# A fused SSM-convolution and gMLP block on one core: the order of work at the passage into the MLP is made anew, and two GpSimd residuals wait for VectorE's first two normalized tiles

## The chip, the cores and the metric

The kernel runs on one core of a Trainium2 chip. A core has five engines with a queue of instructions each: TensorE (PE; its weight loads are shown apart as PEld), VectorE (DVE), ScalarE (ACT), GpSimd (POOL) and SyncE (SP), which here only issues DMAs. The metric is the device time of one execution in microseconds (us). Of a kernel three executions are timed and the median is taken; one more execution is profiled, and its trace is what is read below.

## The reference

The computation is one block with a modulation vector, 2048 positions of 640 channels, in bf16. Cut to what matters:

```python
mod = (silu(c) @ w_mod).reshape(1, 6, 1, -1)          # sa, ca, ga, sb, cb, gb
h = layernorm(x) * (1 + ca) + sa
x = x + ga * A(h, k, v, shift_k, ssm_k, ssm_D)        # short conv of k, times v, long convolution by FFT, times h
h = layernorm(x) * (1 + cb) + sb
x = x + gb * B(h, w_in, w_sp, b_sp, w_out)            # gMLP

def B(x, w_in, w_sp, b_sp, w_out):
    z = gelu(x @ w_in)                                 # 640 -> 1728
    z1, z2 = z[..., :864], layernorm(z[..., 864:])
    g = w_sp @ z2 + b_sp                               # 2048 x 2048 over positions
    return (z1 * g) @ w_out                            # 864 -> 640
```

## The kernel before

The work has three stretches. The first computes part A. The 640 channels are taken in five blocks of 128 (`u` = 0 to 4), the long convolution is a two-stage FFT by matmuls, and every block ends with a product into `gh` and a residual `xt += gh`. The last stretch computes the position mixing (w_sp) and the output projection of part B. Between them lies the passage into the MLP, which the change concerns. Positions are taken there in 16 tiles of 128, four tiles to a group `g`.

For a group the passage does this. The last channel block's outputs arrive from TensorE (`yl`, L875, matmuls of 16 columns). VectorE multiplies them into `gh` (`yml`, L879) and adds `gh` to `xt` (`res`, L831). VectorE takes statistics of `xt` (`ln2`, L837; `ag2`, L968), GpSimd raises the variance to the power -1/2 (`rstd2`, in group 0 `rstdq`, L238), and the tiles are normalized into `Z` (`zx`, L984 to L988, on VectorE, ScalarE or GpSimd). Group 0 goes in two halves of two tiles each; its tiles are turned by TensorE (`hfl`, L1002), five 128x128 blocks a tile, and scaled and shifted out of PSUM by `hmod` (L1014 on ScalarE, L1016 on VectorE). The other groups are turned by a DMA (L1034) and modulated in place (`hmod2`, L1040 and L1042). Then TensorE multiplies by w_in (`zz`, L1060, five accumulating matmuls of 432 columns for each of four outputs of a tile), and ScalarE takes the gelu (L1066) and, for groups 0 and 1, the sum of squares (`zsq`, L1077).

Every operation is recorded with a number; nothing is emitted until the whole program has been recorded. What sets the order is then the table `ORDER` (L51 to L118), written out: each entry is an engine's letter and an operation's number, and `Plan.run` (L149) emits them in this order, so that each engine's queue has its own entries in the order of the table. Tiles' buffers are given out in the same order. Waits between engines follow from what operations read and write. One kind of entry adds a wait: `H` is GpSimd with a gate. A gated operation also waits for the last VectorE operation ahead of it in the table whose kind is in the set `PORT` (L39):

```python
            if e == "D" and o["kind"] in PORT:
                held = made[-1]
            elif gated and held is not None:
                tc.add_manual_dep(made[0], held.name, mybir.DependencyInfo(mybir.DependencyClass.Sync, mybir.DependencyReason.SCHED_ONLY), reason="port")
```

The numbers that matter here: 702 and 759 are the residuals of channel blocks 3 and 4 for group 1 (tiles 4 to 7); 754 is the residual of channel block 4 for tiles 2 and 3; 783 and 784 normalize tiles 0 and 1; 782 is GpSimd's power ahead of them; 785 and 786 are the turns of tiles 0 and 1; 787 to 791 are the `hmod` of the first half; 812, 805, 810 and 829 are the first four groups of `zz` matmuls; 757, 771 and 764 are `yl` of groups 1, 3 and 2. 1040, 1046, 1047 and 1048 are fills (L1112): matmuls of 512 columns whose result nobody reads, two in 1040 and one in each of the others. 590 and 597 are small matmuls for the modulation vector gb. 862 is one of the five `hmod2` of group 1.

## Time and profile before

| | |
|---|---|
| time, median of 3 runs | 303.22 us (303.2 to 303.69) |
| profiled execution: its own time | 303.96 us |
| profiled execution: span, from first to last instruction | 302.2 us |
| PE busy | 292.3 us (97%) |
| VectorE busy | 258.0 us (85%) |
| ScalarE busy | 166.7 us (55%) |
| GpSimd busy | 168.2 us (56%) |
| mean granted TensorE clock | 0.989 of full speed |

A busy share is a mean over stretches with different limits. In the profile's rows an instruction stands with its start in us from the span's start, its duration, its engine, line, operation, what it writes and reads, and, in brackets, how long its engine stood idle before it and what ended that. Rows of equal instructions are merged (x3). Durations of instructions that follow each other overlap by their latency, so that the distance of starts is the better price of one.

### The profile page before, as it was taken

How to read it: one execution, taken by the hardware profiler on the slowest of the kernel's cores; microseconds unless marked ns; L12 is line 12 of the kernel's file. 1: busy time of each engine (PE TensorE's matmuls, PEld its weight loads, DVE VectorE, ACT ScalarE, POOL GpSimd, SP SyncE). 2: the span in 40 equal slices, each digit the busy share in tenths (PEclk: the TensorE clock that was granted, in tenths of full speed). 3: DMA queues.
4: the chain of work that ended last, by engine and by line, in shares of the span. 5: the costliest groups of instructions: out<-in, count | busy, mean ns of one | idle time of the engine just before them, and what ended most of it. 6: DMA issues, size and time to landing. Idle time of an engine off the chain costs nothing.

```text
span 302.2 us, 7173 instructions
## 1 busy us (share of the span) xinstructions
PE 292.3 (97%) x2833; PEld 207.1 (69%) x2833; DVE 258.0 (85%) x541; ACT 166.7 (55%) x325; POOL 168.2 (56%) x192
## 2 busy tenths in 40 slices
PE   6799999999999999799999999999999999999996
PEld 3689999999999988655555555555555555665664
DVE  8999999999998999979887877977678787687895
ACT  6899999997898866159789578310111102111110
POOL 3652768938767988554520521067841655487850
PEclk9999999999999999779999999999999999999999
DMA  8999789995466978005596930049756547332424
GB/s 161 284 230 275 154 221 264 133 229 144 91 121 116 280 126 276 2 2 104 152 209 126 188 74 1 0 90 172 141 138 85 103 112 161 83 85 74 102 68 128
DMA packets 117155, 41.57 MB, mean 138 GB/s; under 512 B 102557, under 2 KB 117122, under 8 KB 117122
## 3 DMA queue, kind: packets, MB, share of 16 engines
q1 hardware_dynamic: 116968, 41.08, 62.6%
q8 instruction: 22, 0.36, 0.5%
q14 instruction: 11, 0.09, 0.1%
q10 hardware_dynamic: 154, 0.05, 0.1%
HBM read 16.60 MB, written 2.63 MB: 64 GB/s over the span
## 4 chain that ended last, share of the span: by engine, by line
PE 90%; DVE 7%; issue 1%; ACT 1%; POOL 0%; DVEq 0%; POOLq 0%
PE ps L1172 24%; PE pu L295 22%; PE pz L295 18%; PE sm L295 7%; PE po L1381 7%; PE s L295 5%; PE po L1394 3%; PE pz L1172 2%; PE pu L1172 1%; DVE Tf L515 1%; DVE T L396 1%; PE sm L654 1%; PE sm L423 1%; DVE st L837 1%; DVE xt L831 1%
## 5 line engine op out<-in xcount | busy, mean ns | idle before, releaser
L295 PEld LDWEIGHTS <-Z 128*128 128x128 bf16 x320 | 31.7, 100 | 28.0 <-issue 1.7
L295 PE MATMUL pu<-X,M 128*128 128x128 bf16 (+1 forms) x480 | 46.2, 237 | 0.4 <-DVE Tf L515 0.3
L529 POOL TENSOR_TENSOR W<-Tf 128x256 bf16<-128x256 f32 x42 | 30.1, 734 | 17.2 <-DVE Tf L515 8.6
L1172 PEld LDWEIGHTS <-S 128*128 128x128 bf16 x256 | 25.0, 98 | 20.8
L295 PEld LDWEIGHTS <-M 128*128 128x128 bf16 x480 | 36.5, 98 | 3.1 <-issue 0.7
L298 ACT CAST X<-s 128x1024 bf16<-128x1024 f32 x32 | 32.7, 1022 | 2.8 <-PE s L295 2.6
L295 PE MATMUL pu<-big,Z 128*128 128x432 bf16 x160 | 33.6, 353 | 0.0
L295 PE MATMUL pz<-big,Z 128*128 128x432 bf16 x160 | 33.5, 353 | 0.0
L515 DVE TENSOR_TENSOR Tf<-pu,KH 128x1024 f32<-128x1024 f32 x25 | 30.4, 1218 | 0.8 <-ACT Z L298 0.4
L1172 PEld LDWEIGHTS <-wT 128*128 128x128 bf16 x192 | 18.8, 98 | 15.3
L1178 ACT COPY m<-ps 128x432 f32<-128x432 f32 x7 | 3.6, 517 | 46.1 <-PE ps L1172 46.1
L295 PEld LDWEIGHTS <-G 128*128 128x128 bf16 x330 | 25.0, 98 | 1.9 <-issue 0.3
L298 ACT CAST KH<-pu 128x512 bf16<-128x512 f32 x40 | 23.5, 605 | 4.2 <-PE pu L295 3.6
L298 ACT CAST Z<-pz 128x512 bf16<-128x512 f32 (+1 forms) x41 | 23.3, 587 | 4.3 <-PE pz L295 4.2
L1172 PE MATMUL ps<-X,wT 128*128 128x432 bf16 x112 | 22.7, 346 | 0.0
L1172 PE MATMUL ps<-X,S 128*128 128x432 bf16 x112 | 22.6, 346 | 0.0
L1172 PE MATMUL ps<-T,S 128*128 128x432 bf16 x112 | 22.2, 346 | 0.0
L1180 ACT ACTIVATE m<-ps,bcol 128x432 f32<-128x432 f32 x7 | 4.3, 621 | 30.2 <-PE ps L1172 30.2
L295 PEld LDWEIGHTS <-X 128*128 128x128 bf16 x288 | 17.8, 98 | 4.4 <-issue 1.8
L295 PE MATMUL sm<-dg,big 128*128 128x128 bf16 x320 | 20.5, 219 | 0.0
L515 DVE TENSOR_TENSOR T<-pu,KH 128x1024 bf16<-128x1024 f32 x15 | 18.3, 1220 | 2.3 <-PE pu L295 2.2
L295 PEld LDWEIGHTS <-big 128*128 128x128 bf16 x320 | 18.8, 98 | 0.3
(235 smaller groups left out, 668.5 us busy)
## 6 DMA issues: line engine op xcount, KB each, us to landing
wm<-in_w_mod_dram SPq DMA_DIRECT2D x6, 800.0 KB, 5.0
xt<-in_A_q_dram SPq DMA_DIRECT2D x4, 640.0 KB, 5.9
out_dram<-ot SPq DMA_DIRECT2D x15, 160.0 KB, 2.0
big<-in_B_w_in_dram SPq DMA_DIRECT2D x2, 1080.0 KB, 8.1
X<-in_A_ssm_k_dram SPq DMA_DIRECT2D x4, 512.0 KB, 7.3
ZT<-in_A_v_dram SPq DMA_DIRECT2D x1, 1024.0 KB, 7.7
big<-in_A_v_dram SPq DMA_DIRECT2D x1, 1024.0 KB, 7.8
w_o<-in_B_w_out_dram SPq DMA_DIRECT2D x6, 160.0 KB, 2.9
```

The lines of the kernel that those rows point to most:

```text
L295: nc.tensor.matmul(o, lhsT=w, rhs=x, start=start, stop=stop)
L298: (e.copy if e is nc.scalar else e.tensor_copy)(dst, src)
L396: e.tensor_scalar(tl[a][:, h], tl["mbase"][:], mstep[:, h * NCH + i:h * NCH + i + 1], MAGIC, op0=ALU.add, op1=ALU.add)
L423: e.transpose(pt[:, i, :], flatM[:, 8 * b + i, :], ident[:])
L515: e.tensor_tensor(T_[:], (tl[pu] if src is None else tl[src])[:, :, :, None, :].to_broadcast(shape), tl[KH][:, :, None, :, :].to_broadcast ...
L529: e.tensor_tensor(tl[W][:, :, o, :], T_[:, :, 0, o, :], T_[:, :, 1, 1 - o, :], op=ALU.add if o else ALU.subtract)
L654: e.transpose(p_[:, i, :], tl[kvt][:, c0 + i, :], ident[:])
L1172: nc.tensor.matmul(ps[:, :FC], lhsT=lhs[:, s_, :], rhs=rhs(s_), start=(s_ == 0 and not more), stop=(s_ == HT - 1), skip_group_check=more)
L1178: e.copy(part[p, m][:], part[p, BANK[m]][:, :FC])
L1180: e.activation(part[p, m][:], part[p, BANK[m]][:, :FC], ACT.Identity, bias=T["bcol"][:, p + HT:p + HT + 1], scale=1.0)
L1381: nc.tensor.matmul(ps[:, :HS], lhsT=w(k), rhs=x(k), start=start and k == 0, stop=stop and k == n - 1, skip_group_check=True)
L1394: e.matmul(po[t, i][:, :hi - lo], lhsT=uTs[t][:fsz[ft], ft, :], rhs=T["w_o"][:fsz[ft], ft, lo:hi], start=(ft == 0), stop=(ft == NFT - 1))
```

## The change

Only the table `ORDER` changes. In three groups of lines between the last channel block and the second group of the MLP, entries are put in another order; two of them also change their letter, from `G` to `H`: 702 stands behind D783 now, and 759 behind D784. Those two are of the kind `zx`, which is in `PORT`, so residual 702 waits for the normalization of tile 0 and residual 759 for that of tile 1. Of the diff a few lines, since its rows only list numbers:

```diff
@@ ORDER @@
-P731 P737 D740 G677 P727 D732 D738 D698 P741 P743 P746 P748 D699 P745 P744 A728 P747 P742 D749 D750 D751 P1046 P1047
-P1048 D752 P757 D780 P1040 S589 D781 P590 D753 D758 D754 P771 G782 D783 D784 G702 D756 A591 P597 A598 D701 P785 P786
-D787 A791 A790 D788 P764 D789 G759 P812 D755 D700 D793 D792 D704 P805 A813 D705 D762 S779 P829 D724 A806 G794 D795
+P731 P737 D740 G677 P727 D732 D738 D698 P741 P743 P746 P748 D699 P745 P744 A728 P747 P742 D749 D750 D751 P1046 P757
+P1047 P1048 D752 D780 S589 D781 P590 D753 D758 D754 P771 G782 D783 H702 D784 H759 D756 A591 P597 P1040 A598 D701 P785
+P786 D787 A790 A791 D788 P764 D789 P812 D755 D700 D793 D792 D704 P805 A813 D762 S779 D724 A806 D763 G794 D795 D761
...
-A828 D768 D707 D769 D708 D653 D710 D654 S599 S858 P820 A821 A809 P825 A826 D859 D860 D861 A832 P817 D863 D909 A814
+A828 D768 D707 D769 D708 D653 D710 D654 S599 S858 P820 A821 P825 A826 A809 D859 D860 D861 A832 P817 P833 A818 A834
```

On GpSimd at the residuals of group 1 the rows ahead and behind keep their order; `rstd` is the power -1/2, and the semaphores that an instruction waits for stand in brackets. Before:

```order
L831 TENSOR_TENSOR xt<-xt,gh 128x4x128
L238 TENSOR_TENSOR rstd_83<-mv_82,mhalf 128x2 [waits DVE_49]
L831 TENSOR_TENSOR xt<-xt,gh 128x4x128
L831 TENSOR_TENSOR xt<-xt,gh 128x4x128 [waits DVE_49]
L236 TENSOR_SCALAR rstd_83<-mv_82 128x2 [waits DVE_49]
L238 TENSOR_TENSOR rstd_83<-rstd_83,mhalf 128x2 [waits Pool_49]
```

And now:

```order
L831 TENSOR_TENSOR xt<-xt,gh 128x4x128
L238 TENSOR_TENSOR rstd_83<-mv_82,mhalf 128x2 [waits DVE_49]
L831 TENSOR_TENSOR xt<-xt,gh 128x4x128 [waits DVE_49] x2
L236 TENSOR_SCALAR rstd_83<-mv_82 128x2 [waits DVE_49]
L238 TENSOR_TENSOR rstd_83<-rstd_83,mhalf 128x2 [waits Pool_49]
```

The first residual behind the power had no wait of its own; now both wait for VectorE, the first for 783 and the second for 784.

On TensorE ahead of the turns of tiles 0 and 1 (L1002, `Z`): `vcol` is operation 597, `s<-ident` with 512 columns a fill, `wm` the small matmuls of operation 590. Before, the two fills of 1040 stand ahead of 590:

```order
L295 MATMUL pz<-Ebd,X 128x4x4
L295 LDWEIGHTS ident
L295 MATMUL s_2843<-ident 128x512
L295 LDWEIGHTS wm
L295 MATMUL sm<-sc_bf,wm 128x1
...
L295 LDWEIGHTS vcol
L295 MATMUL sm<-ident,vcol 5x128
L1002 LDWEIGHTS Z
L1002 MATMUL s_2924<-ident,Z 128x128
```

And now they stand directly ahead of the turns:

```order
L295 LDWEIGHTS vcol
L295 MATMUL sm<-ident,vcol 5x128
L295 LDWEIGHTS ident
L295 MATMUL s_2919<-ident 128x512
L1002 LDWEIGHTS Z
L1002 MATMUL s_2925<-ident,Z 128x128
```

The 32 matmuls of 757 have moved ahead of two of the three single fills, and the pair 1040 has moved behind 597.

On VectorE a few statistics change places around the residuals' readers (`gsa_bf` is an addition into `gh`; `nmr` is the bias for the second half's normalization), and one `hmod2` of group 1, 862, comes over from ScalarE:

```order
 L968 BN_AGGR mv_82<-st_72 128x2 x2
-L837 BN_STATS st_72<-xt 128x6 x3
-L776 TENSOR_TENSOR gh<-gh,gsa_bf 128x4x128
+L837 BN_STATS st_72<-xt 128x6 x2
+L776 TENSOR_TENSOR gh<-gh,gsa_bf 128x4x128
+L837 BN_STATS st_72<-xt 128x6
 L974 SCALAR_TENSOR_TENSOR nmr_84<-mv_82,rstd_83 128x2
...
-L1042 TENSOR_SCALAR Z<-Z,cb_col,sb_col 128x4x128 x4
+L1042 TENSOR_SCALAR Z<-Z,cb_col,sb_col 128x4x128 x5
```

One of the three statistics ahead of the addition now stands behind it, and the in-place modulation of group 1 is five rows of VectorE instead of four. On TensorE 810 also goes ahead of 829, and on ScalarE gelus and sums of squares of group 0 and 1 change places among themselves. No instruction is added or removed.

## The prediction, written before the changed kernel ran

> **What bounds the kernel now.** The page comes first: the granted clock by slices of 7.6 us, and what the chain that ended last consists of.

> ```profile
> span 302.2 us, 7173 instructions
> ...
> PEclk9999999999999999779999999999999999999999
> PE 90%; DVE 7%; issue 1%; ACT 1%; POOL 0%; DVEq 0%; POOLq 0%
> ```

> TensorE sets the end nearly everywhere. The 7% of VectorE are a place where TensorE waits, and the clock falls in just two slices, from 121 to 136 us. So the second view is the chain of waits in order of time around there.

> ```profile
> 124.11 1.23 DVE xt L831
> 125.34 1.20 DVE Z L988
> 126.54 0.05 issue
> ...
> 127.84 0.84 PE sm L295 x32
> 128.68 1.81 PE pz L295 x5
> 130.49 3.63 PE pu L295 x15
> 134.13 0.17 PE s L1002 x3
> ...
> 134.68 2.74 PE pz L295 x15
> ...
> 145.63 0.91 PE pu L295 x5
> ```

> Behind these 0.05 us of issue the chain stays on TensorE until its last matmul, so a microsecond won there is one at the end if no input becomes late. Two losses stand in these rows. The first: fifteen `zz` matmuls take 3.63 us (0.242 each) at 130.49 and 2.74 us (0.183 each) at 134.68. The second: VectorE's residual and normalization take 1.23 and 1.20 us. The third view, the timeline by engine, shows what is unusual in that.

> ```profile
> 121.99 0.29 DVE L831 TENSOR_TENSOR xt<-xt,gh 128x256 bf16<-128x256 bf16 x1
> 124.11 1.23 DVE L831 TENSOR_TENSOR xt<-xt,gh 128x256 bf16<-128x256 bf16 x1
> 125.27 1.62 DVE L988 TENSOR_SCALAR Z<-xt,mv,rstd 128x640 bf16<-128x640 bf16 x2
> 148.31 1.51 DVE L988 TENSOR_SCALAR Z<-xt,mv,rstd 128x640 bf16<-128x640 bf16 x4
> 124.04 2.31 POOL L831 TENSOR_TENSOR xt<-xt,gh 128x512 bf16<-128x512 bf16 x2
> 126.59 0.50 PE L1002 MATMUL s<-ident,Z 128*128 128x128 bf16 x3 [1.64 <-DVE Z L988]
> ```

> The same residual took 0.29 us at 121.99, when GpSimd was idle, and 1.23 at 124.11. Two normalizations should take 0.76 (1.51 us for four) and took 1.62. GpSimd's two residuals (702 and 759) ran from 124.04 to 126.35, right behind the power, 1.16 us each. VectorE's residual ended as the first of them did (125.2), and the first normalization as the second. GpSimd holds something that both engines need for a whole instruction, and TensorE stands idle for 1.64 us. The fourth view is the granted clock by stretches.

> ```profile
> 118.53:121.94 3.41, 3.36 (x67) 2.81 (x65) 3.27 (x9) 2.23 (x4) 2.69 (x3) 1.00 0.54 191
> 121.94:125.36 3.42, 3.01 (x94) 2.55 (x91) 3.32 (x11) 0.42 (x2) 2.00 (x3) 1.00 0.02 5
> 125.36:128.77 3.41, 2.18 (x43) 2.05 (x44) 3.10 (x8) 0.84 (x2) 0.99 (x1) 0.50 0.00 0
> 128.77:132.18 3.41, 3.41 (x11) 1.45 (x10) 3.41 (x15) 0.80 (x3) 2.07 (x4) 0.50 0.00 0
> ```

> The clock (ahead of the last two columns) is half for two stretches of 3.41 us, 125.36 to 132.18. What came before it:

> ```profile
> 121.35 0.81 PE L295 MATMUL s<-ident 128*128 128x512 bf16 x3
> 122.00 0.95 PE L295 MATMUL pz<-Ebd,X 128*128 128x16 bf16 x32
> 122.80 0.59 PE L295 MATMUL s<-ident 128*128 128x512 bf16 x2
> 123.23 0.76 PE L295 MATMUL sm<-sc_bf,wm 128*128 128x1 bf16 x25
> 123.86 0.94 PE L295 MATMUL pz<-Ebd,X 128*128 128x16 bf16 x32
> ```

> At full clock 432 columns take 0.183 us, 0.42 ns each. In 121.94 to 125.36 stand 64 x 16, 2 x 512, 25 and 128 columns (the `vcol` turn): 2,201 columns, 0.93 us, 27% of the stretch, although TensorE counts as busy for 3.01 of it. My reading is that the clock follows what streams through in such a stretch: after 27% it fell.

> **The change part by part.** *The held residuals.* 702 and 759 no longer start behind the power but behind normalizations 783 and 784. Residual 754 then takes 0.29 instead of 1.23 (124.11 to 124.40), and the normalizations 0.38 each: 783 ends at 124.83, 784 at 125.20. With the 0.05 us of issue seen at 126.54, the turns of tile 0 can start at 124.88 and those of tile 1 at 125.25. Before, tile 0's began at 126.59, and tile 1's normalization ended at 126.89 (125.27 + 1.62). Does 702 get between 783 and 784? It is released at 783's end plus some 0.08, at 124.91, and 784 has issued by 124.79, so I take 784 first; the other end is a rival below. The new waits cost nothing there: 702 runs 125.2 to 126.35, 759 to 127.5. Behind them on GpSimd stands the power for the second half.

> ```profile
> 126.81 0.60 DVE L837 BATCH_NORM_STATS2 st<-xt 128x6 f32<-128x128 bf16 x2
> 127.72 1.05 DVE L1016 TENSOR_SCALAR Z<-s,cb_col,sb_col 128x256 bf16<-128x256 bf16 x3 [0.31 <-issue]
> 129.66 0.19 POOL L236 TENSOR_SCALAR rstd<-mv 128x2 f32<-128x2 f32 x1 [3.31 <-DVE mv L968]
> 127.93 1.02 ACT L1014 ACTIVATE Z<-sm,sb_col,cb_col 128x256 bf16<-128x256 bf16 x2 [2.68 <-PE sm L1002]
> 132.85 0.91 ACT L984 ACTIVATE Z<-xt,nmr,rstd 128x640 bf16<-128x640 bf16 x1
> ```

> That power waited 3.31 us for VectorE; 1.9 us earlier it would start at 127.8, behind 759's 127.5. VectorE's readers of the two residuals (statistics of tiles 4 to 7) come about 128.0. Does GpSimd now hold up the `hmod` of the first half, from 125.8 on? They read PSUM. The gauge is VectorE's copies out of PSUM at 119.26 beside two GpSimd residuals:

> ```profile
> 119.26 1.31 DVE L298 COPY X<-pz 128x512 bf16<-128x512 bf16 x3
> 119.42 2.27 POOL L831 TENSOR_TENSOR xt<-xt,gh 128x512 bf16<-128x512 bf16 x2 [0.47 <-DVE gh L793]
> ```

> 0.42 us each, no stretching, so nothing below; the upper bound is that the hmods wait until 127.5, 1.7 us, which gives the gain back.

> *TensorE's rows ahead of the turns.* 1040 moves behind 597. With `yl` 757 earlier, 757, two fills, 590, 771 and 597 end at 121.57 + 0.80 + 0.43 + 0.63 + 0.80 + 0.06 = 124.3, by the distances of starts above, and the two fills at 124.73, 0.15 before the turns may start. So they cost nothing; without that cover at most 0.43 us. They do change the stretch 121.94 to 125.36: 4 x 512, 49 x 16, 153 and about seven turns of 128 are 3,900 columns, 1.64 us, 48% instead of 27%.

> *The sum with the clock kept.* Turns of tile 1 from 125.25 at 0.056 a block (0.17 for three at 134.13): done 125.53. `hmod`: VectorE has its two statistics until 125.80, then three at 0.35, until 126.85; ScalarE's two 125.62 to 126.65. `yl` 764: 0.84, until 126.4. The first `zz` group's third matmul waits for 126.85, and the group ends at 126.9 + 3 x 0.183 = 127.45, before at 130.49. Then fifteen at 0.183: 130.2, before 134.13. **Gain 3.9 us.** Kept in sight for the second half: the power there (127.8) and VectorE's bias behind it let ScalarE's normalization of tile 2 start at about 129.1, and with its 0.91 it ends at 130.0, so TensorE's arrival at 130.2 just holds.

> *The sum with the clock lost again* from 125.36. For one stretch: turns end 125.7, `yl` 126.55, five matmuls at 0.363 until 128.4, one more, then fourteen at 0.183: 131.3, gain 2.8. For two, until 132.18: ten and a half at 0.363, the rest at 0.183: 133.0, gain 1.1.

> Which? 48% lies between 27%, after which the clock fell, and the stretch ahead of it, 118.53 to 121.94, after which it did not. Its groups (the view by lines, for that stretch alone):

> ```profile
> L853 PE MATMUL pu<-ident,Z 128*128 128x128 bf16 x16 | 1.6, 219 | 0.0
> L853 PE MATMUL pz<-ident,Z 128*128 128x128 bf16 x16 | 1.5, 219 | 0.0
> L295 PE MATMUL sm<-Ebd,X 128*128 128x16 bf16 x32 | 1.1, 170 | 0.0
> ```

> Of these 32 turns four began before the stretch; 28 x 128, 32 x 16 and the three fills of 121.35 are 5,632 columns, 69%. I take kept, since the lowest stretch anywhere in the new order stays at about 40%, at some distance from 27%.

> [...]

> *What is moved besides.* 810 ahead of 829, and gelus and squares among themselves: same work on engines that follow TensorE, nothing. 862 costs VectorE another 0.34 (four took 1.37) and spares ScalarE one instruction:

> ```profile
> 143.17 1.37 DVE L1042 TENSOR_SCALAR Z<-Z,cb_col,sb_col 128x512 bf16<-128x512 bf16 x4
> ```

> Group 1's first matmul at 145.63 needs them. VectorE is 1.9 us early at its first `hmod` (125.80 for 127.72) and waits less at the second turns, up to 3.9; I take 3.2, an estimate between these. Then it comes to 143.17 at 140.0, and five end at 141.7; TensorE comes at 141.7, and needs the fourth 0.55 later. No loss, but little left. No DMA moves in its queue.

> **The rivals.** *Clock lost for one stretch*: 303.96 - 2.8 = 301.2. For it: the limit lies unseen between 27 and 69%. *For two*: 302.9. Against it: its second stretch would be full of `zz`, and after such a one (128.77 to 132.18) the clock came back. *The gate does not do what it says*: 702 gets in between 783 and 784, since GpSimd's residual did take its place between normalizations elsewhere:

> ```profile
> 135.98 1.99 DVE L988 TENSOR_SCALAR Z<-xt,mv,rstd 128x640 bf16<-128x640 bf16 x3
> 136.14 1.29 POOL L831 TENSOR_TENSOR xt<-xt,gh 128x512 bf16<-128x512 bf16 x1 [1.65 <-DVE nmr L974]
> ```

> Three took 1.99 instead of 1.13, so it got in behind the first. There it was released 0.08 us after the first had begun. Here it is released at 783's end; if that beats 784, tile 1 ends at 126.4, 0.5 before now, TensorE idles as before and the clock falls: 303.4. *Slower*: the held residuals become the new wait. VectorE is in order; if its statistics of tiles 5 and 6 wait for them, the second half's normalizations are late, and TensorE waits at the second turns. That begins when 759 ends behind 128.4 instead of 127.5 and first eats the gain of 3.9; past 132.3 it is slower, and with 1 us more 304.9. GpSimd's residuals took at most 1.29 here, so two would not reach it.

> **How the numbers follow.** Profiled time 303.96, span 302.2, so 1.76 around it. Clock kept: 303.96 - 3.9 = **300.1**, 55%. That execution stands 0.74 above the median of 303.22; if this is not the clock's place in time but the profiling, the result is 299.3, and a late input of 0.6 makes 300.7: the own range. One stretch 25%; two 8%; the gate failing or `hmod` held 8%; slower 4%. Range 299.1 to 302.9: it takes in the kept clock and both cases of a lost one; the last two cases, 12%, lie beyond, and some 4% lie below. Within 0.2% of the median (302.6 to 303.8, about what can be told from no change) lie the fourth case and part of the third: faster 0.85, same 0.10, slower 0.05.

> **What would show it.** GpSimd's two residuals behind 125; VectorE's 128x256 residual at 124.1 in 0.3 us and two normalizations in about 0.8; TensorE's gap ahead of L1002 under 0.4 instead of 1.64; granted clock 1.00 throughout 121 to 136; the matmuls of group 1 from about 141.7. Wrong if VectorE's rows stay at 1.2, if the clock is at half for 3.4 us or more behind 125, or if a new gap stands at the second L1002 or at group 1.

## The result: 300.61 us against 303.22

| | before | changed |
|---|---|---|
| median (lowest to highest), 9 runs each | 303.22 us (302.89 to 304.42) | 300.61 us (300.24 to 303.14) |
| ratio of the times, 95% interval | | 0.992 (0.9893 to 0.9946) |
| profiled execution: time, span | 303.96, 302.2 us | 301.79, 300.0 us |
| mean granted clock of it | 0.989 | 0.994 |

The kernel is faster, by 2.6 us in the median; the prediction was 300.1, range 299.1 to 302.9. The nine executions fall into three groups, which the granted clock of each tells apart: five with 1.000 (300.24 to 300.61 us), three with 0.993 or 0.994 (301.39 to 301.79), one with 0.989 (303.14). These are the prediction's cases of the clock kept (300.1), lost for one stretch of 3.41 us (301.2) and lost for two (302.9). Below, the clock counts as kept at 0.999 or 1.000. Before, it was always lost: of the 47 executions whose clock was read 24 lost it for one stretch (0.993 or 0.994, median 303.12 us) and 23 for two (0.989, median 304.10). The profile of before, from which the prediction took its sums, is one that lost two; so the 0.74 us by which it stands above the median, which the prediction left open, come from the clock and not from profiling. The changed kernel's profiled execution lost one. Its page, from the span to the chain that ended last:

```profile
span 300.0 us, 7173 instructions
...
PEclk9999999999999999899999999999999999999999
...
PE 91%; DVE 6%; issue 1%; ACT 1%; POOL 0%; DVEq 0%; POOLq 0%
```

One slice shows a little less than full clock where two stood at 7. Around the passage, the timeline of VectorE, GpSimd and TensorE of the changed kernel:

```profile
124.65 0.28 DVE L831 TENSOR_TENSOR xt<-xt,gh 128x256 bf16<-128x256 bf16 x1
124.86 0.80 DVE L988 TENSOR_SCALAR Z<-xt,mv,rstd 128x640 bf16<-128x640 bf16 x2
...
125.38 2.39 POOL L831 TENSOR_TENSOR xt<-xt,gh 128x512 bf16<-128x512 bf16 x2 [0.77 <-DVE Z L988]
...
118.86 0.40 PE L853 MATMUL pu<-ident,Z 128*128 128x128 bf16 x4
124.84 0.27 PE L295 MATMUL sm<-ident,vcol 128*5 128x128 bf16 x1
125.04 1.03 PE L295 MATMUL s<-ident 128*128 128x512 bf16 x2
126.13 0.48 PE L1002 MATMUL s<-ident,Z 128*128 128x128 bf16 x3
294.10 3.05 PE L1394 MATMUL po<-w_o,uT 128*128 128x320 bf16 x28
```

The residual is back at 0.28 us (1.23 before), the two normalizations at 0.80 (1.62), and GpSimd's two residuals follow them. The 1.64 us in which TensorE stood idle ahead of the turns (L1002) are gone. In their place stand the two fills that the change moved there, and they ran at half clock, 1.03 us instead of 0.6. The clock, by stretches:

```profile
121.42:124.83 3.41, 3.41 (x111) 2.95 (x107) 3.31 (x13) 0.47 (x2) 1.52 (x2) 1.00 0.02 5
124.83:128.24 3.41, 3.35 (x50) 2.38 (x47) 2.35 (x9) 1.05 (x3) 2.39 (x2) 0.50 0.00 0
128.24:131.66 3.42, 3.42 (x20) 1.76 (x19) 3.02 (x13) 2.35 (x7) 2.04 (x4) 1.00 0.00 0
```

One stretch at half instead of two, and it follows a stretch in which TensorE was busy without a break.

Executions of one kernel begin the passage up to 0.6 us apart (the first turn of the last channel block, L853, started at 117.71 and at 118.30 us in two profiles of the gates alone). So parts are compared from marks inside each profile: **A**, from that first L853 row to the first L1002 row, and **B**, from there to the start of the last 28 output matmuls (L1394). Before, these marks are at 118.31 and 296.28:

```profile
118.31 0.40 PE L853 MATMUL pu<-ident,Z 128*128 128x128 bf16 x4
296.28 3.05 PE L1394 MATMUL po<-w_o,uT 128*128 128x320 bf16 x28
```

With the 126.59 that the prediction quotes, A = 8.28 and B = 169.69 us. In the changed kernel's execution above A = 126.13 - 118.86 = 7.27 and B = 294.10 - 126.13 = 167.97: 1.01 us were won ahead of the turns, 1.72 behind them.

### The profile page after: what moved, and what is told of

It is laid out like the page before. It is cut to its first block, busy times and chain, and to the rows that moved or that the text cites. A ratio compares the mean times of both kernels' runs of the same rounds, so it can differ in the third digit from the quotient of the medians.

```text
span 300.0 us, 7173 instructions
## 1 busy us (share of the span) xinstructions
PE 292.4 (97%) x2833; PEld 207.5 (69%) x2833; DVE 257.7 (86%) x542; ACT 166.0 (55%) x324; POOL 168.1 (56%) x192
## 4 chain that ended last, share of the span: by engine, by line
PE 91%; DVE 6%; issue 1%; ACT 1%; POOL 0%; DVEq 0%; POOLq 0%
PE ps L1172 24%; PE pu L295 21%; PE pz L295 18%; PE sm L295 8%; PE po L1381 7%; PE s L295 5%; PE po L1394 3%; PE pz L1172 2%; PE pu L1172 1%; DVE Tf L515 1%; DVE Z L639 1%; DVE T L396 1%; PE sm L654 1%; PE sm L423 1%; DVE T L398 0%
## 5 line engine op out<-in xcount | busy, mean ns | idle before, releaser
L295 PEld LDWEIGHTS <-Z 128*128 128x128 bf16 x320 | 31.2, 98 | 26.9 <-DVE Z L1016 0.2
L295 PE MATMUL pu<-X,M 128*128 128x128 bf16 (+1 forms) x480 | 46.3, 237 | 0.4 <-DVE Tf L515 0.3
L295 PEld LDWEIGHTS <-M 128*128 128x128 bf16 x480 | 36.5, 98 | 3.1 <-issue 0.6
L298 ACT CAST X<-s 128x1024 bf16<-128x1024 f32 x32 | 32.7, 1022 | 2.8 <-PE s L295 2.6
L295 PE MATMUL pz<-big,Z 128*128 128x432 bf16 x160 | 32.7, 347 | 0.0
L295 PE MATMUL pu<-big,Z 128*128 128x432 bf16 x160 | 32.6, 346 | 0.0
L295 PEld LDWEIGHTS <-G 128*128 128x128 bf16 x330 | 25.0, 98 | 1.9 <-issue 0.3
L298 ACT CAST KH<-pu 128x512 bf16<-128x512 f32 x40 | 23.5, 605 | 4.2 <-PE pu L295 3.9
L298 ACT CAST Z<-pz 128x512 bf16<-128x512 f32 (+1 forms) x41 | 23.3, 587 | 4.3 <-PE pz L295 4.2
L295 PE MATMUL sm<-dg,big 128*128 128x128 bf16 x320 | 21.1, 223 | 0.3 <-DVE Z L639 0.3
L295 PEld LDWEIGHTS <-X 128*128 128x128 bf16 x288 | 18.1, 99 | 3.2 <-DVE X L453 1.1
L295 PEld LDWEIGHTS <-big 128*128 128x128 bf16 x320 | 19.5, 100 | 1.0 <-issue 0.5
```

The costliest lines, as they stand in the source:

```text
L295: nc.tensor.matmul(o, lhsT=w, rhs=x, start=start, stop=stop)
L298: (e.copy if e is nc.scalar else e.tensor_copy)(dst, src)
```

## Experiments

The experiments assign a part of the gain to each edit and set the prediction's theory against its rivals. The theory: GpSimd's residuals shut VectorE out, the gates end that, and the clock then depends on how many columns TensorE streams in a stretch of 3.41 us. Rivals: the new order brings the gain; the clock falls because of the idle gap or of the late turns.

### The two gates alone

The order of before; only the residuals 702 and 759 moved and gated.

```diff
-... G782 D783 D784 G702 D756 ...   D789 G759 P812
+... G782 D783 H702 D784 H759 D756 ...   D789 P812
```

> The order of before, with only the two gates: residual 702 behind normalization 783, residual 759 behind 784. My theory: the gates alone take GpSimd off VectorE's way, so residual 754 takes 0.3 us instead of 1.23, the two normalizations about 0.8 instead of 1.62, and the turns of tile 1 start about 1.85 us earlier. The two fills stay at their old place, so the stretch that holds the small matmuls keeps a share of 27 to 35% of streamed columns, and the clock falls in most executions, for one stretch of 3.41 us rather than two, since zz follows sooner: 301.2 to 302.0 us median, with few executions at 300.4. Rival (the gain of the change is the clock, and the gates only matter through it): about 303 us as before. Rival (only a gap in TensorE's work lets the clock fall; with the gap closed it stays): 300.3 us, and clock 1.00 in nearly every execution.

Measured: 299.81 us (299.4 to 300.27, 6 runs), ratio 0.9877 (0.9853 to 0.9901), clock 0.999 or 1.000 in all six. Run again later beside the change: 300.2 (300.0 to 300.41, 5 runs), ratio 0.9903 (0.9882 to 0.9924), clock kept in all five. I had expected the clock to fall here; it never did. That is what the rival foretold by which only a gap in TensorE's work lets the clock fall; against that rival stands the changed kernel, which lost the clock without a gap of TensorE over 0.06 us. TensorE's timeline in the second of these:

```profile
118.30 0.40 PE L853 MATMUL pu<-ident,Z 128*128 128x128 bf16 x4
...
122.79 0.59 PE L295 MATMUL s<-ident 128*128 128x512 bf16 x2
123.22 0.76 PE L295 MATMUL sm<-sc_bf,wm 128*128 128x1 bf16 x25
123.85 0.94 PE L295 MATMUL pz<-Ebd,X 128*128 128x16 bf16 x32
124.72 0.22 PE L295 MATMUL sm<-ident,vcol 128*5 128x128 bf16 x1
124.88 0.34 PE L1002 MATMUL s<-ident,Z 128*128 128x128 bf16 x3
...
292.32 3.05 PE L1394 MATMUL po<-w_o,uT 128*128 128x320 bf16 x28
```

A = 6.58 and B = 167.44: 1.70 and 2.25 us less than before, 3.95 in all. The turns follow the `vcol` matmul without a gap. The whole gain is in the gates, and these executions lie below the change's. The 3.95 us are counted from a profile of before that lost two stretches; the medians of the same runs fell from 303.95 to 299.81 and from 303.26 to 300.2.

### The new order alone

The change with `G702` and `G759` in place of `H702` and `H759`.

> The order of the change, without the two gates (702 and 759 start behind the power as before). My theory: VectorE's stall stays (residual 754 1.2 us, two normalizations 1.6), turns of tile 0 start at about 126.6, TensorE idles 1.2 us instead of 1.64 because the two fills fill 0.43 of it, and with 48% of columns in place of 27% the clock falls somewhat less often: 302.0 to 303.2 us median. If the new order were the cause of the gain: 300.6. If the order costs something and the gates pay for it: over 303.5.

Measured: 303.58 us (303.08 to 304.54, 12 runs), ratio 0.9998 (0.9981 to 1.0016); the clock fell in all twelve, to 0.994 or 0.989. The chain of waits around the passage:

```profile
124.14 1.22 DVE xt L831
125.36 1.20 DVE Z L988
126.56 0.05 issue
126.61 0.50 PE s L1002 x3
```

The stall of before, row for row. The new order by itself is worth nothing. The expectation's 302.0 to 303.2 was missed: the two fills in the stall did not make the clock fall less often.

### Where the gate stands

The gates alone, with 702 held behind VectorE's residual 754, one step earlier.

```diff
-G782 D783 H702 D784 H759
+G782 H702 D783 D784 H759
```

> The order of before with the two gates only, but GpSimd's residual 702 is issued and held one step earlier: behind VectorE's residual 754, and no longer behind the normalization 783. By the lock theory (a GpSimd residual of two operands in SBUF shuts VectorE's SBUF work out for its whole 1.15 us) residual 754 keeps 0.28 and 783, issued 0.04 after it, still goes ahead of 702, but 784 is caught behind 702: the turns of tile 1 come about 1.1 us late, TensorE gets a gap near 1 us before its transpositions L1002, and the clock can fall again. Time 300.9 to 302.5, against 299.8 for the kernel with the gate one step later. If 702 gets in ahead of 783, both normalizations are late and the time is that of before, 303.2 to 304. By the rival (what a GpSimd residual costs depends on what lies beside it in all, not on which instruction is issued first) the gate's place by one step changes nothing: 299.6 to 300.2.

Measured: 301.09 us (300.24 to 302.41, 6 runs), ratio 0.9922 (0.9899 to 0.9945), the clock lost in two of six. Timeline of GpSimd, VectorE and TensorE:

```profile
124.47 1.28 POOL L831 TENSOR_TENSOR xt<-xt,gh 128x512 bf16<-128x512 bf16 x1 [0.41 <-DVE xt L831]
...
124.11 0.29 DVE L831 TENSOR_TENSOR xt<-xt,gh 128x256 bf16<-128x256 bf16 x1
124.31 1.63 DVE L988 TENSOR_SCALAR Z<-xt,mv,rstd 128x640 bf16<-128x640 bf16 x2
...
124.88 0.34 PE L1002 MATMUL s<-ident,Z 128*128 128x128 bf16 x3
125.99 0.34 PE L1002 MATMUL s<-ident,Z 128*128 128x128 bf16 x3 [0.66 <-DVE Z L988]
```

The time is within the expectation. 783 had begun 0.16 us ahead of 702 and was not stretched, since the turns of tile 0 came at 124.88 as with the gates one step later. 784 came after 702 and waited for its end: two normalizations took 1.63 us instead of 0.80, and TensorE stood idle for 0.66 us ahead of tile 1's turns. So between these instructions the order of issue decided which engine waited, and for the whole of the other's instruction (1.28 us here).

### One gate instead of two

The gates alone, with `G759` in place of `H759`.

> The order of before with the gate of residual 702 alone; 759 stands behind it in GpSimd's own queue with no gate. Since GpSimd takes its instructions in order, 759 can't begin before 702, and 702 ends 1.15 us after 784: the second gate should do nothing, 299.6 to 300.1 as with both. Were 759's own wait what matters (it is issued beside something that 702 doesn't wait for), the time would lie above 300.5.

Measured: 300.02 us (299.57 to 300.17, 5 runs), ratio 0.9883 (0.9867 to 0.9898), clock kept in all five: as with both, and as expected. 759 stands behind 702 in GpSimd's own queue, so the second gate does nothing.

### The old places of the fills

First the change with the pair 1040 back ahead of 590, but 757 left where the change put it:

```diff
-... D781 P590 ...   A591 P597 P1040 A598
+... D781 P1040 P590 ...   A591 P597 A598
```

> The change, with the two fills of 1040 back at their old place ahead of the small matmuls 590. Same columns, other place. My theory (the clock follows the share of columns in stretches of 3.41 us whose place drifts from execution to execution): the lowest stretch now lies from about 123.2 on, without the fills, some 30% instead of 40, so the clock falls in more of the executions than in the change (4 of 9 there): median 300.8 to 301.6. Rival (the place of the fills is nothing): the same mixture as the change, median 300.3 to 300.7, 40 to 50% of executions with a clock under 1.00.

Measured: 300.3 us (300.24 to 300.58, 6 runs), ratio 0.9894 (0.9871 to 0.9917), clock kept in all six, against my expectation. Six executions beside the change's 4 losses in 14 are too few to show that this place keeps the clock better. In TensorE's timeline the four fills stand together now:

```profile
122.39 1.24 PE L295 MATMUL s<-ident 128*128 128x512 bf16 x4
123.47 0.77 PE L295 MATMUL sm<-sc_bf,wm 128*128 128x1 bf16 x25
```

They occupy 1.08 us, 0.22 more than four times 0.216 (the median distance of starts of matmuls of 512 columns in the profile of before): the second pair is a new tile in a pool with one buffer (`s1`), right behind the last matmul into the old one. The trace shows what it waits for: its first matmul carries a wait for a semaphore that the last matmul into the old tile raises. That one started at 122.61 and ended at 122.98, and the next started at 123.04, 0.43 later instead of 0.22.

Then the change with 757 and the fills 1046, 1047, 1048 and 1040 all in their old places, which leaves the two gates and the rest of the new order:

> The change with TensorE's fills 1046, 1040 and the copy 757 at the places they had before: the two gates and the rest of the new order (statistics, 810, 829, 862, the gelus). By the theory of the streamed share (the clock falls after a stretch of 3.41 us in which at most about 35% of the columns that could be streamed were streamed, and stays at 38% and more) it behaves as the two gates alone: the lowest stretch before 125 has 42 to 44%, the clock is kept in nearly every execution, 299.6 to 300.0. By the rival (the rest of the new order costs the 0.5 to 0.8 us by which the change lies above the gates alone) 300.2 to 300.7, and with the clock kept.

Measured: 300.18 us (299.5 to 300.39, 6 runs), ratio 0.9887 (0.9871 to 0.9904), clock kept in all six; A = 6.57 (124.95 - 118.38). The median lies between the expectation (299.6 to 300.0) and its rival (300.2 to 300.7) and decides nothing; the marks do. A + B is 174.05 us here and 174.01 with one gate, so the rest of the new order neither costs nor gains within what can be told.

### The fills behind 597: none, and four

> The change, with operation 1040 emitting nothing: the two fill matmuls, whose result nobody reads, are left out. My theory: 1,024 columns less, lowest stretch 20 to 27%, the clock falls in nearly every execution for one stretch or two: median 301.2 to 302.5. [...]

Without the two fills (1040 emits nothing, which the result doesn't need): 301.13 us (299.93 to 302.94, 9 runs), ratio 0.9925 (0.9896 to 0.9953). The clock was lost in six of nine, less often than expected. The profiled execution kept it, and the longest gap of TensorE in its passage was 0.29 us, ahead of the turns; so a gap of that length did not by itself take the clock.

> The change with four matmuls in place of two in fill 1040, behind 597 as the change has it. Share theory: two more matmuls of 128x512 are 0.43 us, 12 points of a stretch of 3.41, so the lowest stretch before 125 rises from about 35% to over 40% and the clock is kept in all or nearly all executions; the turns behind the fills come up to 0.43 later. Median 300.4 to 301.0, the single executions nearer together than the change's 300.2 to 303.1. By the rival (whether the clock falls hangs on the gap of TensorE or on its early jitter, not on what is streamed) it falls as often as in the change, 4 times in 9, and the median is 300.8 to 301.5.

With four: 301.96 us (300.12 to 302.04, 6 runs), ratio 0.9929 (0.9904 to 0.9954). The clock was lost in four of six, against my expectation. The fills stand too late for what I wanted of them. In this kernel's profile the emptiest 3.41 us lie from 120.33 to 123.74, and the four fills begin only at 123.90.

### The stall kept, and filled

The order of before without gates. Fill 1040 has seven matmuls instead of two and stands between 597 and the turns, where TensorE waits in any case; 1048 moves behind 757. Two more matmuls go into 1044 and 1045, which stand ahead of the first L853 row, so ahead of mark A. That is seven more in all (the expectation says eight), and between L853 and the small matmuls stand three fills instead of five.

```diff
-FILLS = ((4,), (2,), (2,), (2,), (1, 1, 1), (1, 1, 1))
+FILLS = ((4,), (7,), (2,), (2,), (1, 2, 2), (1, 1, 1))
-P1048 D752 P757 D780 P1040 S589 ...   A591 P597 A598
+D752 P757 D780 P1048 S589 ...   A591 P597 P1040 A598
```

> The kernel before, its order and its stall unchanged (no gates), with eight more fill matmuls of 128x512: two more ahead of the small matmuls, and seven behind 597 where five of them replace nothing, so that TensorE streams 1.5 us of the 1.64 us in which it waits for the late normalization. This takes the clock's part out of the stall and leaves the wait itself. By the reading of the prediction (the stall costs some 1.1 us of waiting, and up to 2.8 us through the half clock behind it) the turns stay where they were, the clock stays at 1.00 in most executions, and the time is 301.0 to 301.8. By the rival (the half clock is no consequence of TensorE's idling, it only goes along with the late turns) the clock falls as before and the time stays 303.0 to 304.2. If the fills make the turns late, 301.8 to 302.5 with the clock kept.

Measured: 302.38 us (301.53 to 303.22, 12 runs), ratio 0.9965 (0.9948 to 0.9982). The clock was kept in eight of twelve (301.53 to 302.44) and lost in four (302.46 to 303.22). Before, it was kept in none of 47. The profiled execution kept it; VectorE's and TensorE's rows:

```profile
124.69 1.23 DVE L831 TENSOR_TENSOR xt<-xt,gh 128x256 bf16<-128x256 bf16 x1
125.84 1.63 DVE L988 TENSOR_SCALAR Z<-xt,mv,rstd 128x640 bf16<-128x640 bf16 x2
...
117.61 0.59 PE L295 MATMUL s<-ident 128*128 128x512 bf16 x2
...
118.28 0.59 PE L295 MATMUL s<-ident 128*128 128x512 bf16 x2
...
125.03 1.68 PE L295 MATMUL s<-ident 128*128 128x512 bf16 x7
127.17 0.34 PE L1002 MATMUL s<-ident,Z 128*128 128x128 bf16 x3 [0.46 <-DVE Z L988]
...
294.69 3.05 PE L1394 MATMUL po<-w_o,uT 128*128 128x320 bf16 x28
```

The first L853 row is at 118.94 here, so A = 8.23 as before (8.28) and B = 167.52 (169.69). This takes the stall apart: late turns cost 1.7 us (8.23 against 6.57), the half clock behind them 2.2, for the two lost stretches of the profile of before. The rival by which late turns bring the half clock falls, since the turns are as late and the clock mostly stayed. Whether it is the gap or the missing columns that counts, this run can't tell, since the fills took away both.

The level of 301.0 to 301.8 that I had expected was missed all the same: the median lies 0.6 above it, and the eight executions that kept the clock lie at 302.1 on average. The passage begins 0.63 us later than in the profile of before, and 0.43 of that are the two added matmuls ahead of it (x2 in the rows at 117.61 and 118.28, where before has one each at 117.41 and 117.86). Without these 0.43 the executions that kept the clock would average 301.7, an estimate, and lie in the expected range.

### The change again, beside the gates alone

> The change itself once more, beside the two gates alone on the same chip. 300.2 to 303.1 in single executions, the clock kept in about half of them, median 300.3 to 301.4.

> The two gates alone once more: 299.4 to 300.3, the clock kept in nearly all executions, median 299.8; 0.4 to 1.4 below the change in the same call. If the difference of the first call was chance, both agree within 0.2.

On one chip, the change: 300.45 us (300.3 to 300.54, 5 runs), clock kept in all five; the gates alone: 300.2, as given above. The expected distance of 0.4 to 1.4 was missed, since the change lost no clock here. The two ranges overlap, so the distance of 0.25 is no proof by itself. The profiles show where it would come from. The change with the clock kept:

```profile
118.63 0.40 PE L853 MATMUL pu<-ident,Z 128*128 128x128 bf16 x4
...
124.62 0.22 PE L295 MATMUL sm<-ident,vcol 128*5 128x128 bf16 x1
124.77 0.60 PE L295 MATMUL s<-ident 128*128 128x512 bf16 x2
125.43 0.33 PE L1002 MATMUL s<-ident,Z 128*128 128x128 bf16 x3
...
292.88 3.05 PE L1394 MATMUL po<-w_o,uT 128*128 128x320 bf16 x28
```

A = 6.80 and B = 167.45. Against the gates alone the change loses 0.22 us ahead of the turns and nothing behind. From the fills to the turns are 0.66 us, twice 0.216 and 0.23: the same extra as with the fills in one row, since the turns write a new tile of that pool, too.

### All parts together

| kernel | median, us | A | B | clock lost | emptiest stretch | positions under 37% |
|---|---|---|---|---|---|---|
| before | 303.22 | 8.28 | 169.69 | 47 of 47 | 8% | 100% |
| new order alone | 303.58 | 8.27 | 169.24 | 12 of 12 | 20% | 100% |
| gate one step early | 301.09 | 6.57 | 169.86 | 2 of 6 | 25% | 61% |
| change, no fills 1040 | 301.13 | 6.50 | 167.56 | 6 of 9 | 27% | 69% |
| change | 300.61, 300.45 | 7.27, 6.80 | 167.97, 167.45 | 4 of 14 | 34% | 24% |
| change, four fills | 301.96 | 7.23 | 167.45 | 4 of 6 | 34% | 24% |
| stall filled | 302.38 | 8.23 | 167.52 | 4 of 12 | 34% | 24% |
| gates alone (both times, one gate, old fills) | 299.81 to 300.2 | 6.57 or 6.58 | 167.44 to 167.48 | 0 of 22 | 35% | 3 or 4% |
| change, 1040 ahead of 590 | 300.3 | 6.79 | 167.47 | 0 of 6 | 35% | 1% |

The last two columns are worked out from the trace: the columns of all matmuls that start within 3.413 us, by 0.417 ns each, as a share of it. (The medians of the distance of starts in the profile of before, 56 ns at 128 columns and 216 at 512, differ by that for each column.) The stretches follow each other without a break (by the clock records, before, 35 at full clock, 2 at half and 50 at full; in the change 34 at full and 1 at half) and lie elsewhere in each execution. Shifting them over all positions gives the emptiest stretch that one of them could meet, and the share of positions in which at least one of them streams under 37%. (For the change this is from the profile that kept the clock. The profiles of before, the new order alone and the early gate lost it, so matmuls behind the loss stand wider apart there.) The limit was chosen after the runs; with any from 36 to 38% no entry moves by more than some 4 points.

Where the stretches really lay is known for the thirteen profiled executions, from the times at which the clock changed. It fell behind a stretch of 27% (before), 34% (change), 35% (new order alone) and 39% (early gate). Where it stayed, the lowest stretch of the passage had 38% (no fills 1040), 39% (four fills), 40% (change) and 42 to 49% (the other six).

## Why the prediction was right, point by point

**The stall and the gates**: right, with its numbers. VectorE's residual 0.28 us (0.29 predicted), two normalizations 0.80 (0.76), GpSimd's residuals behind them, no gap ahead of L1002. That the gates and nothing else do it is shown by the two parts run alone. Tile 0's turns came 1.71 us earlier relative to the mark with the gates alone (8.28 to 6.57), as predicted (126.59 to 124.88).

**That 784 gets ahead of 702**: right. Moved one step earlier, the gate lets 702 in between and costs what the prediction feared in kind, but less: 301.09 in the median, not 303.4, because only tile 1's turns were late (a gap of 0.66 us, not 1.64) and the clock was kept in four of six.

**`hmod` not held by GpSimd**: right. VectorE's three `hmod` beside GpSimd's residuals took 1.05 us, as before, and the second half's power waited for VectorE, not for the residuals. VectorE and GpSimd in the change with the clock kept:

```profile
126.13 1.05 DVE L1016 TENSOR_SCALAR Z<-s,cb_col,sb_col 128x256 bf16<-128x256 bf16 x3 [0.18 <-issue]
...
125.15 2.40 POOL L831 TENSOR_TENSOR xt<-xt,gh 128x512 bf16<-128x512 bf16 x2 [0.77 <-DVE Z L988]
128.07 0.19 POOL L236 TENSOR_SCALAR rstd<-mv 128x2 f32<-128x2 f32 x1 [0.52 <-DVE mv L968]
```

The held residuals became no new wait, and the slower rival did not occur.

**The fills cost nothing**: wrong by 0.23 us. The prediction let the two fills end 0.15 before the turns could start. Two rows of its sum were short: from 771 to `vcol` are 0.87 (123.86 to 124.73), not 0.80, and from `vcol` to what follows 0.15, not 0.06. That uses up the 0.15. And it left out the 0.23 between a last matmul into the one-buffer pool and the first into the next tile. In an execution that loses the clock they cost more, since they then run at half speed: 1.09 us from their start to the turns.

**The sum with the clock kept**: predicted 3.9; measured between the marks 8.28 - 6.80 + 169.69 - 167.45 = 3.72 for the change and 3.95 for the gates alone. The difference is the fills.

**The page's 7% of VectorE**: read too narrowly. They are some 21 us of the chain, of which this place holds 2.43 (1.23 and 1.20); another piece, for one, is two instructions of L396 at 8.81, with 1.49 us. The changed kernel's page still has 6%. The sums don't use this share.

**One stretch lost**: predicted 1.1 us worse than the clock kept. The change's two profiles differ by 7.27 - 6.80 + 167.97 - 167.45 = 0.99.

**The clock**: the reading was right, that it follows what is streamed and not how long TensorE idles. In the changed kernel it fell although the trace shows no gap of TensorE over 0.06 us from 117.6 on; with the stall filled it stayed in eight of twelve. By the prediction's own sign of being wrong, a clock at half for 3.4 us behind 125, its profiled execution was the rival of one lost stretch (124.83 to 128.24). The size was off. The prediction took 40% for the emptiest stretch of the new order and called that a distance from 27%. The profiled execution had 34%, from these groups between 121.42 and 124.83 (six of the 83 matmuls of 16 columns began before):

```profile
L295 PE MATMUL pz<-Ebd,X 128*128 128x16 bf16 x64 | 1.9, 169 | 0.0
L295 PE MATMUL s<-ident 128*128 128x512 bf16 x3 | 1.0, 377 | 0.0
L295 PE MATMUL sm<-Ebd,X 128*128 128x16 bf16 x19 | 0.8, 170 | 0.0
L295 PE MATMUL sm<-sc_bf,wm 128*128 128x1 bf16 x25 | 0.8, 163 | 0.0
```

77 x 16 + 3 x 512 + 25 are 2,793 columns, 1.16 us. In the profile that kept the clock the stretches began 0.8 us earlier relative to the work, and the emptiest had 40%, because five turns of L853 fell into it. So one kernel has both outcomes, by where the stretches happen to lie, and a single share was the wrong quantity to predict: 10 kept, 3 with one stretch lost and 1 with two in 14 executions, against chances of 55, 25 and 8%. That the median of the nine came so near to 300.1 is in part luck: five had kept the clock, and with one fewer the median would have been 301.39.

**The rest of the order** (810, 829, 862, statistics, gelus): nothing, as predicted, by the run with the old places of the fills. TensorE's first matmul of group 1 came at 142.23 in the execution that kept the clock, 3.72 earlier than before from the mark, with no new gap.

What stays open: whether the columns are exactly what the clock counts. One execution of the kernel with the early gate fell after a stretch of 39%, where 10 of the matmuls were turns, while others stayed after 38 and 39% with at most three turns in them. So the share alone does not part the two outcomes, and no run shows what else does. Nor is it explained why four of six executions with four fills lost the clock where the positions give one or two.

## What to carry to other kernels

When an instruction of VectorE takes four times its usual duration (1.23 us for 0.29 here), look for a GpSimd instruction that started just ahead of it (here a residual, 0.07 us ahead), and hold that one behind the critical VectorE work: here one gate on one instruction was worth 3.6 us in the median (303.65 to 300.02), and a gate one step too early lost over 1 us of it. Count what TensorE streams in any 3.4 us of a passage, not how busy it looks: here the clock fell to half behind a stretch of matmuls mostly of 1 and 16 columns (34% of what could be streamed) without a gap over 0.06 us. A few wide matmuls that nobody reads, set among them, went with a kept clock (0 of 28 lost); directly ahead of the work that the passage waits for, they delayed it by 0.22 us and the clock was lost in 4 of 14.

## What the runs showed of the hardware

Not expected was the price of a new tile in a pool with one buffer, when it follows right behind the last matmul into the old one: 0.22 and 0.23 us at two places. In the trace it is a wait for the end of that last matmul: with the four fills in one row it ended at 122.98 and the next started at 123.04, and in the changed kernel's profile the last fill ended at 126.08 and the first turn started at 126.13.
